# A new start order, some VectorE copies on ScalarE, earlier bank emptying, and second-layer weights stored already split

## The chip, the cores and the metric

The kernel runs on one core of one Trainium2 chip. The metric is device time in microseconds (us). Three runs of the kernel before took 1604.84 to 1608.25 us, with a median of 1606.85 us. Engines are named as in the profile: PE is TensorE, PEld its weight loads, DVE is VectorE, ACT is ScalarE, POOL is GpSimd, and SP is SyncE, which here only issues DMAs.

## What is computed

For each of 8 batches with 8 heads and 576 positions of 64 numbers, keys and values are first reduced to 32 memory slots, and the attention runs over those slots:

```
a   = softmax(phi over positions)             phi: 8 x 8 x 576 x 32
k_m = a^T k ;  v_m = a^T v                    32 x 64 per head
att = softmax(q k_m^T / 8) v_m                576 x 64 per head
x   = att, heads side by side                 4608 x 512
x   = relu(x w_in)^2 w_out                    first layer, 512 -> 2048 -> 512
h   = x w2_in ;  out = (h - tanh(h)) w2_out   second layer, same sizes
```

The inputs are 64-bit floats, handed over as pairs of 32-bit words.

## The kernel before, in words

**Numbers.** Every 64-bit weight tile of 128x512 is turned into 32-bit floats by `conv` (L131): one DMA of 512 KB into a `raw` (or `wo`) buffer, an ACT absolute value (L142), and four DVE operations (L144 to L148). A factor of a matmul is then split into a rounded high part and the low rest (`split`, L181: an ACT cast, then a subtraction on POOL or DVE), and each product is three matmuls: high by high, high by low, low by high.

**First layer.** Its work is a list of 256 steps (`seq`, L396). A step is one unit `u` of 288 tokens with one 128-row slice `f` of the 2048 hidden features. `step(s)` (L611) issues six matmuls of 128x288 for step s+3 (`l1_mm1`, L410), the relu, square and split for step s+2 (`l1_act`, L422 to L427), and twelve matmuls into four accumulator banks for step s (`l1_mm2`, L439 to L441). The attention is folded into the weights: `u_make` (L275) multiplies v_m into w_in, so that the first matmul takes the attention weights `aT` and the product `u`. At the last slice of a unit's part, `l1_out` (L447) copies the four accumulator banks out to `xs` tiles, two on ACT and two on DVE (L450), and stores or accumulates them to memory. Units 0 to 3 are done in parts of 4, 4 and 8 (or 8 and 8) slices, so that the first steps need few weights.

**What sets the order.** The work beside the steps is written as Python generators: `w..` converts a tile of w_in, `o..` a tile of w_out, `i..` is the memory-slot half of the attention (`att_a`, L198), `j..` the query half (`att_b`, L304), `u..` is `u_make`. Each advances one stage at a time, and each engine's queue is in the order in which the stages are issued. For the start, the order is the written list `ORDER` (L40), one word per stage; `S` in it is one step of the matmul pipeline. Up to about step 60 the list sets the order. After that `tick` (L371) advances every active generator once after each step, those that wait for nothing but emptying a PSUM bank (marked `"-"`) first. Two PSUM banks (`b`) serve all attention and `u_make` matmuls. Generators of batch b begin about 52 steps before its first unit.

**Second weights.** `w2_conv` (L461) converts the 32 tiles of the second layer's weights from step 40 on, one every 5.3 steps, and stores each as 128x512 floats (256 KB) in a memory scratch tensor. Near the end of the first layer `w2_load` (L473) loads each again into a scratch buffer and splits it (`split`, by DVE, for ten tiles by POOL). These loads, their scratch buffers and the loads of the first two token blocks (`x2_load`, L491) share the buffers `f2`, `f` and `raw`; SP issues the DMAs in order, and a DMA that waits for a buffer holds those behind it.

**Second layer.** 144 steps of 9 token blocks by 16 slices (L710): twelve matmuls of 128x512 (`l2_mm1`, L525) for step s+3, the function on ACT and DVE (L537 to L545), the split (L554 on ACT, L555 on POOL), and twelve matmuls for step s (`l2_mm2`, L569 to L571). After a block's last slice four banks are copied by ACT (L576) and stored by SP (L583) in pieces that follow the order of the output rows.

Of the kernel before, what the change touches and what calls it, by code (L numbers as in the profile page):

```python
# [37 lines left out]


ORDER = """  # L40
w22 o12 w02 o11 w10 i00 i01 j11 o2 o1 o3 i00 u01 o0 o6 w00 i01 o8 o0 w00 w02 w10 w02 i00 w00 w02 o0 i21 j00 i00 i00
w10 w01 w03 w13 w23 i00 w20 i00 w02 j01 o0 w03 w31 i00 i00 o9 i01 j01 w02 j01 o0 w01 o0 w01 i00 w00 i00 i00 o2 w03 i10
i01 w00 w10 w02 w12 i00 o4 w03 o0 w00 j01 o1 o12 i01 o0 i01 j01 i01 i20 w03 o1 j01 j01 i01 w01 o15 w13 o2 j00 o3 i01
i01 w01 o2 o2 w03 j00 u01 i01 w03 i01 i01 i01 o1 o4 w21 j01 w01 j01 j01 j01 o13 o12 j00 o1 w12 w00 w31 j01 j01 u00 u00
u00 i10 o7 o12 o2 w11 j20 o1 j00 o2 i10 w11 w30 o1 i11 j01 o4 j01 o3 j00 j01 w13 j00 j11 o1 o12 j01 j00 i11 i11 i10
i11 w31 i10 j00 i10 w11 j00 i10 o4 o12 o2 o12 o3 w10 w13 o4 i10 w03 j00 j00 w11 w12 o12 i10 o5 o5 j00 j00 o4 w01 o3 o4
i10 o4 j10 j00 w12 o14 j00 S j00 w13 i11 i10 i11 S i11 i11 o10 w12 o3 S o3 j11 i11 i10 i10 o5 w13 w00 j11 o3 S i11 o10
S i10 w10 i20 S o6 j11 w11 o4 o8 w32 i11 w11 w32 i11 i11 j11 w33 u10 S o5 o6 o7 j11 o7 j10 j11 j10 j11 o7 S w10 o5 o5
o6 j11 j11 o7 w12 u01 u01 u01 S w12 o5 o7 w20 o5 j11 o7 i20 o6 w02 u10 i20 j11 o8 j11 o10 j10 S u11 o6 u10 j21 j10 j11
w23 j10 o10 o10 w23 w23 o7 j10 o6 j11 j11 j10 S j10 j10 S o2 o8 j10 j10 w22 w22 o10 o8 j20 o6 w23 j10 w22 S w21 w23  # L50
w21 j10 w21 j10 o8 S S w20 w22 j20 j10 o11 w31 j10 S u11 w21 w31 S u11 w22 o8 j20 w21 S j20 S S o11 o9 j20 w20 S o11
w22 o10 o8 o9 o11 o11 o14 w20 o11 w20 o11 o14 w23 S j20 i20 w20 w21 j20 S u02 u02 o10 o9 o9 w23 w20 o13 S o13 u02 o9
u12 w11 o9 o12 w31 o14 j01 o14 u12 o14 S o13 o13 w10 u12 o9 i20 w13 w30 w32 w32 o10 S w32 w32 o13 w30 j20 o14 w22 w31
S w23 S w33 w30 w32 w22 w32 w21 S i21 w22 w23 w30 w33 w32 w30 S w30 w30 i21 i21 i20 i21 i20 S o13 o14 i20 w01 w33 S
w33 w31 i20 o15 i21 i21 w31 w33 S w20 w22 w30 w23 w32 w21 w20 w22 w32 w31 w20 w23 w30 w20 S i20 w32 i21 w33 i21 w20
w31 w31 o15 w21 i21 w30 w20 S i20 u03 w33 i20 u03 i21 S i20 w33 o13 j21 w22 u13 w23 w30 w31 w31 u03 w31 S w20 i21 i21
w22 i20 w31 w30 w30 w31 w31 S i21 w33 w20 w32 S w32 w21 w22 j20 w30 w33 i21 w20 w30 j20 w30 j21 w31 w10 w30 w33 S w23
w22 j21 w23 w20 S w32 w22 j20 i20 o15 w33 w31 w31 w32 i21 w20 w33 w21 o15 j21 w21 S w23 w32 j20 i20 i21 w22 w31 o15
w01 w30 w21 o15 w13 w23 i20 j21 w21 j20 j21 o15 j11 i20 i20 i20 j20 S i20 i21 i20 i20 u13 w21 i20 u13 S i21 i21 j21
j21 j20 i21 S j20 j21 j21 w32 w21 S j20 w33 S S S i20 j20 w21 S i20 w21 i20 i20 w23 w33 j20 i21 w33 j21 S i21 S S j20  # L60
j20 i21 i21 j20 i21 j20 j20 j20 j20 i00 j20 j20 S j21 j20 o6 j21 j20 w22 j21 S j21 w01 w33 j20 j21 w20 j21 j21 j20 i21
j20 j21 j21 j21 j21 j21 i21 j21 j20 j21 j21 j21 j21 j20 j20 S S i21 j01 S S S j21 S w32 S j20 j20 j21 j21 j20 j20 j21
j21 j21 S j21 j21 j21 j21 S j21 j21 S j20 j21 j21 j20 j20 S j20
"""


# [5 lines left out]
def moe_chain_kernel(ctx: ExitStack, tc: tile.TileContext, q, k, v, phi, w1i, w1o, w2i, w2o, out):  # L72
# [43 lines left out]
    def slot(p, shape, name, dt=F32):  # L116
        return p.tile(shape, dt, tag=p.name, name=name)
# [6 lines left out]
    def give(*rs):  # L124
        free.update(rs)
# [72 lines left out]
    def att_a(b, g, p_kv):  # L198
# [21 lines left out]
        yield "-"  # L220
        nc.vector.reduce_max(mx, t[:, :SP], axis=AX.X)
        dg = slot(p_f, [P, P], "dg")
        nc.vector.tensor_scalar(dg, ident, mx, None, op0=ALU.mult)
        give("b")
        yield "b"
        t = psum(ps_b, "mb")
# [36 lines left out]
            kt[b] = slot(a_kt, [P, H, M], f"kt{b}")  # L263
        yield "-"
        ts = t[:, :2 * P].rearrange("p (i h m) -> p i h m", i=2, h=4)
        nc.vector.tensor_copy(kt[b][:, heads], ts[:, 1])
        for o in range(2):
            nc.scalar.copy(vt[b][half(o), 2 * g:2 * g + 2], ts[half(o), 0, o::2])
        give("b")
# [34 lines left out]
    def att_b(b, o, p_q):  # L304
# [8 lines left out]
        for i in (0, 2):  # L313
            yield "b b"
            t = [psum(ps_b, f"qT{i}") for _ in range(2)]
            for n in range(2):
                for c in range(3):
                    nc.tensor.transpose(t[n][:, c * SP:(c + 1) * SP],  # L318
                                        qs[:, i + n, 2 * c:2 * c + 2, :].rearrange("p c d -> p (c d)"), ident[:SP, :SP])
            if i and p_q is a_q:  # L320
                give("q")
            yield "-"
            nc.scalar.copy(qt[:, i], t[0][:, :HT])
            nc.vector.tensor_copy(qt[:, i + 1], t[1][:, :HT])
# [45 lines left out]

    active, wants = [], {}  # L371

    def tick(new=()):
        active.extend(new)
        for gen in sorted(active, key=lambda gen: wants.get(gen, "") != "-"):
            need = collections.Counter(wants.get(gen, "").strip("-").split())
            if any(free[r] < n for r, n in need.items()):
                continue
            free.subtract(need)
            try:  # L380
                wants[gen] = next(gen) or ""
            except StopIteration:
                active.remove(gen)
# [87 lines left out]
    wi, ahead = {}, [3]

    def w2_load(m, f, p, p_x2f):  # L473
        of = "f2" if m == 0 else "f" if f < 8 else "raw"
        yield of
        x = slot(dict(f2=p_x2f, f=p_f, raw=p_raw)[of], [P, 512], "w2f")
        nc.sync.dma_start(x, w2_d[m, f])
        for _ in range(ahead[0]):
            yield
        if m:  # L480
            t = slot(p, [P, 2, 512], "wo", F32R)
            wo[2, f] = t[:, 0], t[:, 1]
        else:
            t = slot(p[f], [P, 2, 512], f"wi{f}", F32R)
            wi[f] = t.rearrange("p t (c n) -> p t c n", c=ET)
        yield from split(x, t[:, 0], t[:, 1], nc.gpsimd if m == 0 and f >= 6 else nc.vector)
        give(of)

    x2 = {}

    def x2_load(j, c, p_x2f):  # L491
        yield "f2 f2"
        ts = [slot(p_x2f, [P, 512], "x2f") for _ in range(2)]
        c0 = 512 * j
        while c0 < 512 * (j + 1):
            u, o = divmod(c0, HT)
# [61 lines left out]
    def l2_mm2(s):  # L558
# [7 lines left out]
        for i in range(4):  # L566
# [110 lines left out]
    for s in range(next_step[0], N1):  # L677
        if s == N1 - 22:
# [68 lines left out]
```

## Time and profile before

| what | value |
|---|---|
| median of 3 runs | 1606.85 us |
| the profiled execution's own time | 1608.32 us |
| its span, first to last instruction | 1606.2 us |
| mean granted TensorE clock | 0.995 |
| PE busy | 1535.8 us (96%) |
| PEld busy | 1334.0 us (83%) |
| DVE, ACT, POOL busy | 1071.6, 848.1, 620.6 us |

Busy time of an engine is the time in which at least one of its instructions is under way. A matmul's entry in the profile includes its way through the array, so successive ones overlap; the distance from one start to the next shows the rate. A wait names the engine, line and tile that waited, and what released it. In waits, the three numbers are the total in us, the count and the longest.

### The profile page before, as it was taken

Reading aid. Unit: us, or ns where it says so; the run is one execution under the profiler, and the core shown is the slowest. Engines: PE = TensorE matmul, PEld = TensorE weight load, DVE = VectorE, ACT = ScalarE, POOL = GpSimd, SP = SyncE. Lnnn points to the kernel's source line nnn. Section 1 sums busy time; section 2 is a strip of 40 time slices with the busy share of each in tenths; the row PEclk is TensorE's granted clock in tenths of the full one; section 3 lists DMA queues with packets and bytes.
Section 4 is the critical chain, followed back from the end, with each engine's and each line's share of the span. In section 5 each row is a group of like instructions: output and inputs, shape, how many; then the busy total and the mean of one; then the engine's idle time right before and its main releaser. Section 6 shows DMA issues by size and latency. Waiting matters only on the chain.

```text
span 1606.2 us, 26164 instructions
## 1 busy us (share of the span) xinstructions
PE 1535.8 (96%) x9904; PEld 1334.0 (83%) x9904; DVE 1071.6 (67%) x1508; ACT 848.1 (53%) x1765; POOL 620.6 (39%) x588
## 2 busy tenths in 40 slices
PE   4588999999999999999999999999999999999998
PEld 2477899998989899999978788888888888888887
DVE  6987445453535535430389788888979888888885
ACT  2466666666666665665755444445444444444443
POOL 2545465543534344443445333232424232333322
PEclk9999999999999999999999999999999999999999
DMA  9546655562644545321431100101010101010000
GB/s 304 161 130 157 212 134 158 152 197 79 208 141 151 174 156 171 109 108 35 122 106 46 42 12 20 34 1 43 11 40 14 41 12 42 11 43 11 19 9 27
DMA packets 89854, 146.28 MB, mean 91 GB/s; under 512 B 12416, under 2 KB 65664, under 8 KB 86656
## 3 DMA queue, kind: packets, MB, share of 16 engines
q1 hardware_dynamic: 86272, 141.07, 28.3%
q0 software_dynamic: 3456, 3.54, 1.7%
q8 instruction: 78, 1.28, 0.3%
q14 instruction: 48, 0.39, 0.1%
HBM read 109.58 MB, written 35.00 MB: 90 GB/s over the span
## 4 chain that ended last, share of the span: by engine, by line
PE 87%; DVE 4%; DMA 4%; ACT 2%; issue 1%; SPq 0%; POOL 0%; ACTq 0%; DVEq 0%; POOLq 0%
PE h L525 23%; PE h L410 12%; PE o L569 8%; PE o L571 8%; PE o L570 8%; PE acc L441 8%; PE acc L439 8%; PE acc L440 8%; PE u L283 2%; PE vkm L244 1%; DMA kv<-in_v 1%; DMA kv<-in_k 1%; PE qT L318 1%; DMA raw<-in_moe_w_out 1%; DMA raw<-in_moe_w_in 1%
## 5 line engine op out<-in xcount | busy, mean ns | idle before, releaser
L525 PE MATMUL h<-x,wi 128*128 128x512 f32 x1728 | 415.4, 390 | 2.1 <-POOL x L508 2.1
L555 POOL TENSOR_TENSOR gl<-pl,gh 128x512 fp32r<-128x512 f32 x144 | 190.3, 1321 | 528.7 <-PE o L570 482.8
L525 PEld LDWEIGHTS h<-x,wi 128*128 128x128 f32 x1728 | 324.1, 188 | 70.2 <-POOL x L508 3.1
L427 POOL TENSOR_TENSOR g<-gg,g 128x288 fp32r<-128x288 f32 x256 | 223.1, 886 | 365.0 <-ACT g L426 277.2
L439 PE MATMUL acc<-g,wo 128*128 128x288 f32 x1024 | 302.1, 295 | 3.4 <-DVE xs L450 3.2
L441 PE MATMUL acc<-g,wo 128*128 128x288 f32 x1024 | 302.7, 296 | 0.0
L440 PE MATMUL acc<-g,wo 128*128 128x288 f32 x1024 | 302.3, 295 | 0.0
L537 ACT ACTIVATE u<-h 128x512 f32<-128x512 f32 x144 | 86.1, 598 | 392.0 <-PE h L525 391.9
L410 PE MATMUL h<-aT,u 128*128 128x288 f32 x1536 | 261.2, 306 | 8.2 <-ACT aT L362 3.5
L410 PEld LDWEIGHTS h<-aT,u 128*128 128x128 f32 x1536 | 218.9, 191 | 41.9 <-issue 21.3
L571 PE MATMUL o<-wo,gl 128*128 128x512 f32 x576 | 225.8, 392 | 2.4 <-POOL gl L555 2.4
L569 PE MATMUL o<-wo,gh 128*128 128x512 f32 x576 | 226.0, 392 | 1.1 <-ACT gh L554 1.1
L570 PE MATMUL o<-wo,gh 128*128 128x512 f32 x576 | 225.6, 392 | 0.0
L439 PEld LDWEIGHTS acc<-g,wo 128*128 128x128 f32 x1024 | 193.2, 189 | 4.1 <-DVE xs L450 3.7
L441 PEld LDWEIGHTS acc<-g,wo 128*128 128x128 f32 x1024 | 193.3, 189 | 0.0
L440 PEld LDWEIGHTS acc<-g,wo 128*128 128x128 f32 x1024 | 193.1, 189 | 0.0
L540 DVE SCALAR_TENSOR_TENSOR pl<-u 128x512 f32<-128x512 f32 x144 | 100.1, 695 | 95.4 <-ACT u L537 95.4
L422 ACT ACTIVATE gg<-h 128x288 f32<-128x288 f32 x256 | 104.9, 410 | 103.7 <-PE h L410 98.3
L544 DVE SCALAR_TENSOR_TENSOR pl<-pl,u 128x512 f32<-128x512 f32 x144 | 148.5, 1031 | 0.0
L545 DVE COPY_PREDICATED pl<-m,th 128x512 f32<-128x512 int32 x144 | 139.0, 965 | 4.9
L571 PEld LDWEIGHTS o<-wo,gl 128*128 128x128 f32 x576 | 108.9, 189 | 26.8 <-POOL gl L555 4.1
L569 PEld LDWEIGHTS o<-wo,gh 128*128 128x128 f32 x576 | 108.7, 189 | 24.5 <-ACT gh L554 1.9
(85 smaller groups left out, 1993.0 us busy)
## 6 DMA issues: line engine op xcount, KB each, us to landing
w<-w_d SPq DMA_DIRECT2D x24, 1024.0 KB, 5.7
raw<-in_moe_w_out SPq DMA_DIRECT2D x32, 512.0 KB, 5.6
raw<-in_moe_w_in SPq DMA_DIRECT2D x32, 512.0 KB, 5.4
kv<-in_v SPq DMA_DIRECT2D x64, 144.0 KB, 4.6
kv<-in_k SPq DMA_DIRECT2D x64, 144.0 KB, 4.3
q<-in_q SPq DMA_DIRECT2D x16, 576.0 KB, 5.6
x_d<-xs SPq DMA_DIRECT2D x64, 144.0 KB, 3.4
w_d<-wf SPq DMA_DIRECT2D x32, 256.0 KB, 2.2
```

What stands on the lines that cost most here:

```text
L410: nc.tensor.matmul(t[:, :HT], uu[:, w, o, c], at[u // 2][:, x, o, u % 2 * HT:u % 2 * HT + HT], start=(n == 0), stop=(n == 5))
L427: nc.gpsimd.tensor_tensor(gl, gg, gh.bitcast(F32), op=ALU.subtract)
L439: nc.tensor.matmul(o, wh[:, c], gh, start=(f == a), stop=False)
L440: nc.tensor.matmul(o, wh[:, c], gl, start=False, stop=False)
L441: nc.tensor.matmul(o, wl[:, c], gh, start=False, stop=(f == z - 1))
L525: nc.tensor.matmul(t, wi[f][:, w, c, :], x, start=(n == 0), stop=(n == 11))
L544: stt(pl, pl, A0, u, op0=ALU.add, op1=ALU.mult)
L545: nc.vector.copy_predicated(pl, m.bitcast(I32), th)
L555: nc.gpsimd.tensor_tensor(lo, pl, hi.bitcast(F32), op=ALU.subtract)
L569: nc.tensor.matmul(o, gh[:, c], wh, start=(f == 0), stop=False)
L570: nc.tensor.matmul(o, gh[:, c], wl, start=False, stop=False)
L571: nc.tensor.matmul(o, gl[:, c], wh, start=False, stop=(f == FT - 1))
```

## The change

Five things change. (1) `ORDER` is a new list: 779 words in place of 716, with the same pieces and 66 `S` in both. (2) Copies move from DVE to ACT: the diagonal `dg` in `att_a` (L223), the `kt` copy (L266), the second `qt` copy (L324), and, for units 0 to 3, the two of four `xs` copies (L450) that DVE had. (3) `empty()` runs between `l1_act` and `l1_mm2` of a step: generators whose next stage empties a PSUM bank are advanced there, ahead of the `xs` copies of a unit's end, and not a second time in the same step's `tick`. (4) `w2_conv` splits the tile where it is converted (ACT cast, DVE subtraction) and stores both parts (512 KB); `w2_load` is one DMA into the final buffer, with no scratch buffer and no split, and ten tiles of each matrix are loaded later; the second token block's `x2_load` takes `raw` buffers in place of `f2`. (5) For the last two output banks, the copy is halved between ACT and DVE, and the second DMA of each bank is issued from ACT.

```diff
--- before.py
+++ after.py
@@ -38,29 +38,31 @@
 
 
 ORDER = """
-w22 o12 w02 o11 w10 i00 i01 j11 o2 o1 o3 i00 u01 o0 o6 w00 i01 o8 o0 w00 w02 w10 w02 i00 w00 w02 o0 i21 j00 i00 i00
...
+w00 w00 o11 w02 i01 o0 w11 i00 u01 o2 w10 o8 w22 o12 j00 i00 i01 w02 w01 w02 i00 o0 i21 i00 i00 o3 j11 o0 w00 i00 w03
...
 """
 
 
@@ -220,7 +222,7 @@
         yield "-"
         nc.vector.reduce_max(mx, t[:, :SP], axis=AX.X)
         dg = slot(p_f, [P, P], "dg")
-        nc.vector.tensor_scalar(dg, ident, mx, None, op0=ALU.mult)
+        nc.scalar.activation(dg, ident, AF.Copy, scale=mx)
         give("b")
         yield "b"
         t = psum(ps_b, "mb")
@@ -263,7 +265,7 @@
             kt[b] = slot(a_kt, [P, H, M], f"kt{b}")
         yield "-"
         ts = t[:, :2 * P].rearrange("p (i h m) -> p i h m", i=2, h=4)
-        nc.vector.tensor_copy(kt[b][:, heads], ts[:, 1])
+        nc.scalar.copy(kt[b][:, heads], ts[:, 1])
         for o in range(2):
             nc.scalar.copy(vt[b][half(o), 2 * g:2 * g + 2], ts[half(o), 0, o::2])
         give("b")
@@ -321,7 +323,7 @@
                 give("q")
             yield "-"
             nc.scalar.copy(qt[:, i], t[0][:, :HT])
-            nc.vector.tensor_copy(qt[:, i + 1], t[1][:, :HT])
+            nc.scalar.copy(qt[:, i + 1], t[1][:, :HT])
             give("b", "b")
         while not {("a", b, g) for g in range(2)} <= done:
             yield
@@ -370,9 +372,22 @@
 
     active, wants = [], {}
 
+    emptied = []
+
+    def empty():
+
+        for gen in [gen for gen in active if wants.get(gen, "") == "-"]:
+            advance(gen)
+            emptied.append(gen)
+            if wants[gen] == "end":
+                active.remove(gen)
+
     def tick(new=()):
         active.extend(new)
+        done_now, emptied[:] = list(emptied), []
         for gen in sorted(active, key=lambda gen: wants.get(gen, "") != "-"):
+            if gen in done_now:
+                continue
             need = collections.Counter(wants.get(gen, "").strip("-").split())
             if any(free[r] < n for r, n in need.items()):
                 continue
@@ -447,7 +462,7 @@
     def l1_out(u, a):
         outs = [slot(p_t, [P, HT], "xs") for _ in range(ET)]
         for e in range(ET):
-            (nc.vector.tensor_copy if e % 2 else nc.scalar.copy)(outs[e], acc[u][e][:, :HT])
+            (nc.vector.tensor_copy if e % 2 and u > 3 else nc.scalar.copy)(outs[e], acc[u][e][:, :HT])
         yield
         for e in range(ET):
             if a:
@@ -456,7 +471,7 @@
                 nc.sync.dma_start(x2_d[u][e], outs[e])
 
 
-    w2_d = {(m, f): p_d.tile([P, 512], F32, name=f"w2_d{m}_{f}") for m in range(2) for f in range(FT)}
+    w2_d = {(m, f): p_d.tile([P, 2, 512], F32, name=f"w2_d{m}_{f}") for m in range(2) for f in range(FT)}
 
     def w2_conv(m, f):
         if m:
@@ -464,33 +479,35 @@
         else:
             src = w2i.rearrange("(c p) f -> p c f", p=P)[:, :, f * 2 * P:(f + 1) * 2 * P]
         x = yield from conv(src, None, None, 3)
-        yield
-        nc.sync.dma_start(w2_d[m, f], x)
+        yield "raw"
+        t = slot(p_raw, [P, 2, 512], "w2s", F32R)
+        yield from split(x, t[:, 0], t[:, 1], nc.vector)
         give("f")
-
-    wi, ahead = {}, [3]
-
-    def w2_load(m, f, p, p_x2f):
-        of = "f2" if m == 0 else "f" if f < 8 else "raw"
-        yield of
-        x = slot(dict(f2=p_x2f, f=p_f, raw=p_raw)[of], [P, 512], "w2f")
-        nc.sync.dma_start(x, w2_d[m, f])
-        for _ in range(ahead[0]):
-            yield
+        yield
+        nc.sync.dma_start(w2_d[m, f], t.bitcast(F32))
+        give("raw")
+
+    wi = {}
+
+    def w2_load(m, f, p):
+        t = slot(p if m else p[f], [P, 2, 512], "wo" if m else f"wi{f}", F32R)
+        nc.sync.dma_start(t.bitcast(F32), w2_d[m, f])
         if m:
-            t = slot(p, [P, 2, 512], "wo", F32R)
             wo[2, f] = t[:, 0], t[:, 1]
         else:
-            t = slot(p[f], [P, 2, 512], f"wi{f}", F32R)
             wi[f] = t.rearrange("p t (c n) -> p t c n", c=ET)
-        yield from split(x, t[:, 0], t[:, 1], nc.gpsimd if m == 0 and f >= 6 else nc.vector)
-        give(of)
+        yield
 
     x2 = {}
 
     def x2_load(j, c, p_x2f):
-        yield "f2 f2"
-        ts = [slot(p_x2f, [P, 512], "x2f") for _ in range(2)]
+        of = "raw" if j == 1 else "f2 f2"
+        yield of
+        if j == 1:
+            t = slot(p_raw, [P, 2, 512], "x2r")
+            ts = [t[:, i] for i in range(2)]
+        else:
+            ts = [slot(p_x2f, [P, 512], "x2f") for _ in range(2)]
         c0 = 512 * j
         while c0 < 512 * (j + 1):
             u, o = divmod(c0, HT)
@@ -507,7 +524,10 @@
         for i in range(2):
             nc.gpsimd.tensor_tensor(lo[:, i], ts[i], hi[:, i].bitcast(F32), op=ALU.subtract)
             x2[j, c + i] = hi[:, i], lo[:, i]
-            give("f2")
+            if j != 1:
+                give("f2")
+            elif i:
+                give("raw")
             yield
 
     N2 = NB * FT
@@ -573,14 +593,20 @@
                 if i % 2 == 0:
                     acc["t"] = slot(p_raw, [P, 2, 512], "osb")
                 t = acc["t"][:, i % 2]
-                nc.scalar.copy(t, o)
+                last = j == NB - 1 and i > 1
+                if last:
+                    nc.scalar.copy(t[:, :256], o[:, :256])
+                    nc.vector.tensor_copy(t[:, 256:], o[:, 256:])
+                else:
+                    nc.scalar.copy(t, o)
                 c0 = 512 * j + P * i
                 a = c0
                 while a < c0 + P:
                     u, r = divmod(a, HT)
                     cc, p0 = divmod(r, SP)
                     n = min(SP - p0, c0 + P - a)
-                    nc.sync.dma_start(out_v[u // 2, 2 * cc + u % 2, p0:p0 + n, :], t[a - c0:a - c0 + n, :])
+                    q_out = nc.scalar if last and a > c0 else nc.sync
+                    q_out.dma_start(out_v[u // 2, 2 * cc + u % 2, p0:p0 + n, :], t[a - c0:a - c0 + n, :])
                     a += n
 
 
@@ -611,6 +637,7 @@
     def step(s):
         l1_mm1(s + 3)
         l1_act(s + 2)
+        empty()
         if s >= 0:
             l1_mm2(s)
 
@@ -683,11 +710,8 @@
             p_x2.append(pool("x2_0", 4, **tile_wise))
             p_wi += [pool(f"wi{f}", 1, **tile_wise) for f in range(6)]
             for f in range(FT):
-                if f < 6:
-                    at_step(s + 2 * f, w2_load(0, f, p_wi, p_x2f))
-                else:
-                    at_step(N1 - 8 + f, w2_load(0, f, p_wi, p_x2f))
-                at_step(N1 - 16 + f, w2_load(1, f, p_wo, p_x2f))
+                at_step(s + 2 * f if f < 6 else N1 - 4 + f, w2_load(0, f, p_wi))
+                at_step((N1 - 15 if f < 6 else N1 - 3) + f, w2_load(1, f, p_wo))
             for c in (0, 2):
                 at_step(N1 - 9 + c, x2_load(0, c, p_x2f))
                 at_step(N1 + 4 + c, x2_load(1, c, p_x2f))
@@ -700,7 +724,6 @@
             p_wi += [pool(f"wi{f}", 1, side="right", **tile_wise) for f in range(FT - 1, 5, -1)][::-1]
         new, plan[s] = plan.get(s, ()), ()
         tick(new)
-    ahead[0] = 1
     tick(plan.pop(N1, ()))
     plan = {k - N1 - 3: g for k, g in plan.items() if k >= N1}
     def l2_ready(s):
```

## Rows read from the trace of the kernel before

**Rows 1.** The page: span, and busy time by engine over the whole span.

```profile
span 1606.2 us, 26164 instructions
...
PE 1535.8 (96%) x9904; PEld 1334.0 (83%) x9904; DVE 1071.6 (67%) x1508; ACT 848.1 (53%) x1765; POOL 620.6 (39%) x588
```

**Rows 2.** Stretches: length, busy us of PE, PEld, DVE, ACT, POOL, granted clock, DMA, GB/s.

```profile
0.00:50.00 50.00, 23.28 (x182) 12.98 (x182) 36.82 (x62) 15.10 (x28) 14.00 (x18) 1.00 0.93 283
50.00:100.00 50.00, 33.21 (x299) 27.79 (x300) 45.61 (x67) 26.66 (x59) 22.18 (x22) 1.00 0.47 151
100.00:150.00 50.00, 43.95 (x333) 38.88 (x332) 39.81 (x58) 31.96 (x73) 34.05 (x33) 0.97 0.54 126
150.00:200.00 50.00, 48.17 (x438) 43.17 (x437) 26.44 (x48) 31.31 (x73) 22.15 (x25) 0.97 0.69 214
250.00:650.00 400.00, 392.28 (x3516) 365.54 (x3515) 186.70 (x298) 248.74 (x571) 173.63 (x198) 1.00 0.50 155
```

**Rows 3.** Waits of PE from 75 to 200 us, first and last of eleven.

```profile
PE acc L439 <- DVE xs L450: 3.2, 2, 2.0
...
PE acc L439 <- ACT xs L450: 0.2, 1, 0.2
```

**Rows 4.** The same view of stretches, two short ones of the start.

```profile
135.00:140.00 5.00, 5.00 (x27) 5.00 (x28) 1.09 (x3) 1.27 (x3) 4.71 (x5) 0.66 1.07 208
160.00:165.00 5.00, 3.53 (x18) 3.07 (x18) 2.74 (x6) 4.71 (x12) 1.61 (x2) 0.81 0.77 233
```

**Rows 5.** Instruction groups by line: count, busy us, mean ns, idle time before; DVE copies.

```profile
L450 DVE COPY xs<-acc 128x288 f32<-128x288 f32 x44 | 19.6, 454 | 78.6 <-PE acc L441 39.0 <-POOL g L427 33.0 <-issue 6.6
...
L324 DVE COPY qt<-qT 128x288 f32<-128x288 f32 x32 | 14.4, 451 | 43.4 <-PE qT L318 43.4
...
L223 DVE TENSOR_SCALAR dg<-ident,mx 128x128 f32<-128x128 f32 x16 | 6.0, 375 | 0.8
L266 DVE COPY kt<-vkmT 128x128 f32<-128x128 f32 x16 | 4.6, 290 | 36.9 <-PE vkmT L259 36.9
```

**Rows 6.** The same view: the other two of the four copies, on ACT.

```profile
L450 ACT COPY xs<-acc 128x288 f32<-128x288 f32 x44 | 17.1, 398 | 33.5 <-PE acc L441 33.5
```

**Rows 7.** One wait of PE over the whole span.

```profile
PE m1T L219 <- DVE u L288: 7.3, 5, 1.5
```

**Rows 8.** Order of time, 365 to 371 us: start, length, instruction, idle time before it.

```profile
365.36 1.09 PE L283 MATMUL u<-w,vt 64*32 64x512 f32 x16
...
368.31 0.46 DVE L450 COPY xs<-acc 128x288 f32<-128x288 f32 x1 [3.31 <-issue]
...
369.00 1.08 ACT L287 CAST u<-u 128x512 fp32r<-128x512 f32 x2
...
370.46 0.28 PE L219 MATMUL m1T<-ident,m 96*128 96x96 f32 x1 [1.46 <-DVE u L288]
```

**Rows 9.** Order of time, PE, where the second layer begins.

```profile
805.90 11.12 PE L525 MATMUL h<-x,wi 128*128 128x512 f32 x48
```

**Rows 10.** The chain that ended last: start, length, what.

```profile
893.03 3.42 POOL x L508 x2
901.57 2.74 PE h L525 x12
...
1587.03 2.72 PE h L525 x12
```

**Rows 11.** Groups by line, DVE: the second weights' subtraction before the second layer.

```profile
L184 DVE TENSOR_TENSOR wo<-w2f,wo 128x512 fp32r<-128x512 f32 x16 | 15.6, 990 | 16.3 <-ACT wo L182 16.3
```

**Rows 12.** DMA issues: KB each, median us to landing.

```profile
w<-w_d SPq DMA_DIRECT2D x24, 1024.0 KB, 5.7
raw<-in_moe_w_out SPq DMA_DIRECT2D x32, 512.0 KB, 5.6
```

**Rows 13.** Order of time, the end of the span: ACT's last copies, SP's last issues.

```profile
1598.63 2.62 ACT L576 COPY osb<-o 128x512 f32<-128x512 f32 x4 [2.85 <-PE o L571]
...
1599.24 4.06 SPq L583 DMA_DIRECT2D out<-osb  x8
```

More of the change, by code (lines that the diff above doesn't have):

```diff
@@ L40 @@
 ORDER = """
-w22 o12 w02 o11 w10 i00 i01 j11 o2 o1 o3 i00 u01 o0 o6 w00 i01 o8 o0 w00 w02 w10 w02 i00 w00 w02 o0 i21 j00 i00 i00
[L42 to L60, printed above, removed]
@@ L61 @@
-j20 i21 i21 j20 i21 j20 j20 j20 j20 i00 j20 j20 S j21 j20 o6 j21 j20 w22 j21 S j21 w01 w33 j20 j21 w20 j21 j21 j20 i21
-j20 j21 j21 j21 j21 j21 i21 j21 j20 j21 j21 j21 j21 j20 j20 S S i21 j01 S S S j21 S w32 S j20 j20 j21 j21 j20 j20 j21
-j21 j21 S j21 j21 j21 j21 S j21 j21 S j20 j21 j21 j20 j20 S j20
+w00 w00 o11 w02 i01 o0 w11 i00 u01 o2 w10 o8 w22 o12 j00 i00 i01 w02 w01 w02 i00 o0 i21 i00 i00 o3 j11 o0 w00 i00 w03
+w20 w02 i00 w02 w00 o3 w10 i00 w01 w01 o0 w03 w03 w12 w10 i00 i01 j01 w02 j00 o1 o2 i00 o0 j00 i01 w00 w02 j01 j01 i20
@@ new lines @@
+w00 w13 i00 i00 i00 o12 w00 w03 o0 o4 w31 o1 i01 i10 i01 o4 w23 o0 j00 o9 j01 i01 w03 o1 j01 i01 j01 w01 w10 j01 o2
+i01 w01 u00 o4 o15 i01 o2 i01 u01 o12 o2 i01 w03 w21 i01 i01 w03 o1 w01 j01 j01 o4 w13 o13 o0 j01 o4 o1 j20 w11 w00
+u00 u00 j01 j01 w11 j01 o2 o4 w21 i00 o6 u00 o2 o12 w11 w21 o1 o3 w12 o4 o1 o4 j01 j00 j00 j01 o1 j00 w30 j00 w31 j00
+w21 o12 o7 j01 i10 j01 i10 i10 o2 i10 w11 j00 i10 i11 o12 j01 o3 o2 j00 i10 o12 i10 w10 j11 w31 w31 i11 o0 w02 j00 o12
+w12 i10 w03 i11 j00 j00 o5 o4 o5 o3 w13 o3 i10 j00 j00 o14 S i10 o10 i11 w12 i11 w13 o5 i10 j00 j11 S i11 w00 w12 i11
@@ new lines @@
+w01 S S o3 i11 w20 w11 o3 i11 i10 o5 i01 i20 j11 o10 o3 S i11 S j11 w13 w10 w11 o7 i10 o7 w13 o7 w32 w00 w32 o6 j11
+w33 o8 i11 i11 o7 i11 u10 S u12 j11 j11 j11 o6 j10 S o7 o5 o7 o5 w10 j11 j11 o6 j10 w12 S u01 o5 j10 u01 o5 j11 w12
+u10 i20 o7 u01 o10 o6 j10 o6 j10 o8 j11 S u11 o7 o6 u10 o10 j11 w23 j01 j11 w21 j21 o6 w23 o10 j10 o1 j10 u12 j11 j11
+j10 S j10 j20 o2 w23 S o8 j10 o10 w23 o8 o12 j10 w21 j10 w01 j10 S o8 w22 j10 j10 w22 S S o11 w20 w22 w21 w23 j10 j10
+S w21 j20 u11 S i20 w21 u11 o8 w22 w02 o11 S j20 S w20 S j20 w31 o11 o10 o1 o10 w22 w22 j20 o9 o14 o11 w11 S o11 w31
@@ new lines @@
+w31 w20 o11 w20 w23 o8 w21 o14 S w20 o9 S u02 j20 i20 u02 w23 w32 o9 o9 j20 w20 o13 S w33 o10 u02 o13 o9 o14 o11 u12
+o9 j01 o14 o12 w23 u12 S j11 o13 o13 u12 w23 o9 i20 w13 w10 w23 w30 w32 w32 o14 w32 S w21 w31 w33 w23 w32 o14 w21 w22
+o13 j20 w30 w30 w23 S i21 w32 S w32 w30 S w33 j01 S i21 i21 i20 w33 w23 w30 i21 w33 w30 w31 w30 w20 i20 S o14 i20 w01
+j20 o13 S w00 w33 w20 w23 i21 w31 i20 w21 w31 w31 w31 o15 w33 w31 S w31 j10 j20 w02 w31 S w22 w30 w30 i20 w22 i21 i21
+w23 w23 j20 o15 S i21 i21 i20 u03 w33 w30 i20 u03 i21 j10 w21 o12 w03 S i20 S w20 i21 i21 i20 u13 w23 w23 o13 j21 u03
@@ new lines @@
+w33 i21 w31 w31 j01 w33 w20 w22 w30 w20 w22 w31 i20 S w20 w32 w32 j20 w20 i21 S w20 j21 j20 w10 j20 w20 j21 w30 w31
+w33 o15 w32 w22 i20 S o14 o2 i21 S w21 i21 w30 w22 w20 w30 w33 w01 o12 w32 w31 w22 w21 j21 o15 w13 S w31 w01 i21 w32
+j20 o15 w21 w20 o15 w32 j10 o15 w30 w30 w21 j21 j20 w22 j21 w33 i10 j11 S w21 w22 w20 j20 w10 u13 w32 w32 u13 w21 w20
+S j20 w31 w32 w22 S w31 w21 w21 j20 S j21 o6 j11 w30 j20 w22 w21 j21 j21 S w31 S S w33 w30 j20 j21 j20 S o15 j20 j01
+j20 j20 j20 i00 j20 w33 S j20 S S w23 j20 o3 j21 j21 i20 j20 j00 j20 j21 S j20 w03 j20 j20 w01 j01 j21 j20 S j20 j21 S
@@ L64 @@
+i20 w32 o0 j20 w20 j00 j20 j20 S w33 S j21 i21 j21 j21 S i21 j21 j21 i21 j20 j21 w22 S j20 S o7 j21 i20 i21 j21 i20
+j20 j20 i20 i21 S i21 i20 i21 j21 j21 j21 j20 j20 i20 j21 i21 j21 j21 i20 j21 i21 i21 j21 i21 i21 S j21 i20 j21 j21
+i20 w32 j21 j21 S j21 j20 w21 w33 S j21 S i20 j20 w11 i20 j21 j21 j21 j21
 """
@@ L466, in w2_conv @@
         x = yield from conv(src, None, None, 3)
+        yield "raw"
+        t = slot(p_raw, [P, 2, 512], "w2s", F32R)
+        yield from split(x, t[:, 0], t[:, 1], nc.vector)
+        give("f")
         yield
-        nc.sync.dma_start(w2_d[m, f], x)
-        give("f")
-    wi, ahead = {}, [3]
-    def w2_load(m, f, p, p_x2f):
-        of = "f2" if m == 0 else "f" if f < 8 else "raw"
-        yield of
-        x = slot(dict(f2=p_x2f, f=p_f, raw=p_raw)[of], [P, 512], "w2f")
-        nc.sync.dma_start(x, w2_d[m, f])
-        for _ in range(ahead[0]):
-            yield
+        nc.sync.dma_start(w2_d[m, f], t.bitcast(F32))
[4 more added lines that the diff above has]
+        nc.sync.dma_start(t.bitcast(F32), w2_d[m, f])
         if m:
-            t = slot(p, [P, 2, 512], "wo", F32R)
             wo[2, f] = t[:, 0], t[:, 1]
         else:
-            t = slot(p[f], [P, 2, 512], f"wi{f}", F32R)
             wi[f] = t.rearrange("p t (c n) -> p t c n", c=ET)
-        yield from split(x, t[:, 0], t[:, 1], nc.gpsimd if m == 0 and f >= 6 else nc.vector)
-        give(of)
+        yield
     x2 = {}
     def x2_load(j, c, p_x2f):
-        yield "f2 f2"
-        ts = [slot(p_x2f, [P, 512], "x2f") for _ in range(2)]
+        of = "raw" if j == 1 else "f2 f2"
[5 more added lines that the diff above has]
+            ts = [slot(p_x2f, [P, 512], "x2f") for _ in range(2)]
         c0 = 512 * j
```

## The prediction

> **What bounds the kernel now.** I read the page first: PE is busy 96% of 1606.2 us, its weight loads 83%, DVE 67%, ACT 53% [rows 1]. So PE bounds the kernel on average, and a gain has to come from the places where PE stands still or has not started. The view of stretches shows where those are. In the first 50 us PE is busy 23 us, in the next 50 us 33, then 44 and 48; from 250 to 650 us it is busy 392 of 400 [rows 2]. While PE is short of work, DVE is the engine that is full: 37, 46 and 40 of 50 us in the first three stretches, against 15, 27 and 32 for ACT [rows 2]. The list of PE's waits from 75 to 200 us says the same in detail: eleven kinds, 3.2 us for the first and 0.2 for the last, 11.7 us together, and most name a DVE copy [rows 3]. Two short dips of the granted clock come on top: the clock reads 0.66 and 0.81 over 5 us [rows 4], its lower level of 1.2 GHz for a part of each stretch and 2.4 GHz in the rest. The missing shares, 0.34 and 0.19 of 5 us, are 2.6 us of PE time.
>
> The steady first layer has one wait that repeats: the transpose `m1T` waits for the `u` subtraction, five times, 7.3 us [rows 7]. In order of time it is plain why [rows 8]: at a unit's end the `xs` copies stand on ACT and DVE ahead of the `u` cast and subtraction, which empty the two `b` banks. The `u` matmuls end at 366.45, a copy of `xs` starts at 368.31, the casts start only at 369.00, and PE stands still for 1.46 us before `m1T`.
>
> Then the change of layers. PE's first second-layer matmul starts at 805.90 [rows 9]. The steady rate comes from the chain: from 901.57 to 1587.03 lie 126 steps [rows 10], 5.440 us each, so a group of twelve matmuls is 2.72. The group at 901.57 is the eighteenth of L525, with 17 such groups and 14 of the output product ahead of it: 31 x 2.72 = 84.3 us, where 95.7 went by. The change of layers loses 11.3 us, in two places: the first steps, where the splits of the second weights stand between the steps' own DVE work (0.99 us each for a `wo` tile [rows 11]), and a later place where POOL splits the second token block too late, at 893.03 [rows 10].
>
> **The change, part by part.**
>
> *Copies off DVE, and the new list.* Up to about step 31, within the first 200 us, the change takes from DVE: 8 `qt` copies at 0.451, 4 `kt` at 0.290, 4 `dg` at 0.375 and, at six part ends of units 0 to 3, 12 `xs` at 0.454 [rows 5]: 3.6 + 1.2 + 1.5 + 5.4 = 11.7 us. I counted the pieces of both lists: the conversions ahead of each step are nearly the same, so the new list mainly fits the lighter DVE. Where DVE is full, its queue's work is the time: I take 11.7 us, which is also what PE waits after 75 us [rows 3]. Bounds: a loss of 5 us, if the new list orders worse and half of what ACT takes over shows; and a gain of 17.4 us, if all 11.7 us of waits go, the 2.6 us of clock with them, and the four attention halves ahead of the first step start it 3.1 us earlier (4 x 0.451, 2 x 0.290, 2 x 0.375 [rows 5]). On ACT the same copies cost about 28 x 0.4 = 11 us by its own `xs` copy, 0.398 [rows 6]; ACT has 95 us free of the first 200 [rows 2], so this is covered. Without that cover they would sit in front of the relu of the next step, 0.4 us a copy.
>
> Here a rule speaks against the move. The trace has both engines doing the same copy out of a bank: 0.454 us on DVE, 0.398 on ACT [rows 5, 6]. The Trainium skill, "ScalarE: Activation LUTs", Rules for kernel authors, says to use VectorE and not ScalarE for simple element work, DVE being up to about three times faster in bf16 for single-source operations. By that rule the first term would be gone; for this 32-bit copy out of a bank the rows do not agree.
>
> *Banks emptied first.* `empty()` puts the casts and subtractions of [rows 8] ahead of the `xs` copies. The `u` matmuls are done 2.5 us before the casts begin now, so the casts can run ahead of the `xs` copies. Gain 7.3 us [rows 7]; bounds 0 and 7.3. What is late next are the `xs` copies; the next unit's first accumulation needs the first bank only after six more matmuls and `m1T`, about 1 us of cover.
>
> *Second weights split where converted.* Removed at the change of layers: 32 ACT casts, 22 DVE and 10 POOL subtractions, and the sharing of `f2` and `raw`. I expect all 11.3 us back. Bounds: 11.3 and 4, the second being the case that the token block stays late. Added: 32 casts and 32 DVE subtractions, at most 0.99 us each [rows 11], between steps 40 and 214. DVE is idle for 213 and ACT for 151 of the 400 us in the middle [rows 2], so I cost them at nothing; as the pattern (5.3 steps) nearly repeats every 32 steps, a collision with an emptying would repeat in five batches, so the bound is 5 x 0.99 = 5 us. A second `raw` buffer per conversion lengthens its stay; the batches begin 52 steps ahead, which covers it. On SP, stores of 512 KB follow the subtraction by a step and wait for little; the loads of the late tiles stand one of each matrix per second-layer step, issued three steps or more ahead of use. The load of 1024 KB takes 5.7 us [rows 12], so 512 KB is well inside 16 us.
>
> *The end.* ACT's four copies end at 1601.25; SP issues eight stores one after another from 1599.24 for 4.06 us [rows 13]. Two of the eight go to ACT's queue, so SP ends about 2 x 0.5 us earlier, and the half copies save about 0.2; ACT's last half copy stands behind one issue, which takes 0.1 back. I take 1.1 us, bounds 0.4 and 1.7.
>
> **Sum.** 11.7 + 7.3 + 11.3 + 1.1 = 31.4 us. The profiled execution took 1608.3 us itself, 2.1 more than its span, and 1.5 us over the median 1606.85; less 31.4 it is 1576.9, or 1575.4 from the median. I say 1576.
>
> **The rivals.**
> - *The start gives nothing.* If ACT, DMA or the latency from stage to stage sets the start, the first term is 0: 1588 us. For it: DMA is 0.93 busy in the first 50 us [rows 2], and PE waits there for chains across engines. Against it: DVE is 91% busy from 50 to 100 us [rows 2]. By the rule of the Trainium skill above the time would be this one too.
> - *The layers' change stays late.* If the second block's split or the loads still come late, 7 to 11 us stay: about 1585.
> - *The wait moves.* `xs` copies behind the casts hold the next unit's accumulation for as long as `m1T` waited: 7.3 us less, 1583.
> - *Slower: the doubled loads starve the second layer.* Twenty loads of 512 KB, two per step, are due in its first ten late steps. A 512 KB load took 5.6 us in the crowded start [rows 12]. If they land one after another at that price, two cost 11.2 us against a step of 5.44: 5.8 late per step, 58 in ten steps, less three steps of lead, 16: 42 us late, 1618 us. It decides from 2.72 us per load upwards. Against it: the median of 1024 KB is 5.7 us [rows 12], and DMA moved 283 GB/s in the first 50 us [rows 2], which is 1.9 us for 512 KB.
> - *The parts do nothing.* If DVE's relief is taken up by added splits in the middle (5 us), `m1T` stays and the layers' change gains only 4: about 1607, no change.
>
> **How the numbers follow.** Forecast 0.62, a start without gain 0.18, a late change of layers 0.07, a moved wait 0.06, slower 0.04, nothing 0.03. At the one end, 17.4 + 7.3 + 11.3 + 1.7 = 37.7, which is 1569 from the median; 1566 leaves room for an earlier first step than I can price. At the other end, no gain at the start and every other part at its lower half, 7.3 - 5 + 7 + 0.4 = 9.7, is 1597; what is worse is left out with the slower case and the last one. A measurement of this kernel can tell about 0.2% (3.2 us) from no change. Faster by more than that: 0.93; within it: 0.03; slower: 0.04.
>
> **What would show it.** Right: the waits of `acc` for `xs` and of `m1T` for `u` are gone; the first steps of the second layer are 5.44 us apart at once, and POOL ends no wait there; DVE is busy some 12 us less in the first 200 us, and the first-layer steps stand 10 us or more earlier by 280 us. Wrong: a new wait of PE for ACT's copies (`qt`, `xs`, `dg`) in the first 200 us, second-layer matmuls that wait for a DMA, or a first step no earlier than before.

## The result and the profile after

The changed kernel takes 1582.11 us (median of 4 runs, 1580.14 to 1583.17), the kernel before 1607.55 beside it. The ratio is 0.9841 with a 95% interval of 0.9823 to 0.9860: 25.4 us, or 1.6%, faster. Beside other kernels it was measured once more at 1581.0 us, with a ratio of 0.9834 (0.9818 to 0.9849).

The page of the kernel after, span and busy time, as in [rows 1]:

```profile
span 1578.4 us, 26135 instructions
...
PE 1523.9 (97%) x9904; PEld 1329.9 (84%) x9904; DVE 1043.0 (66%) x1436; ACT 868.1 (55%) x1849; POOL 605.2 (38%) x578
```

Its stretches, with the columns of [rows 2]:

```profile
0.00:50.00 50.00, 21.49 (x182) 12.89 (x182) 33.61 (x57) 19.02 (x39) 12.51 (x18) 1.00 0.84 276
50.00:100.00 50.00, 38.10 (x346) 31.95 (x340) 42.12 (x64) 32.27 (x76) 29.33 (x28) 1.00 0.51 158
100.00:150.00 50.00, 42.95 (x338) 38.11 (x338) 39.69 (x48) 33.85 (x79) 31.15 (x31) 0.97 0.65 158
150.00:200.00 50.00, 48.50 (x453) 45.50 (x453) 24.96 (x40) 35.23 (x86) 24.48 (x28) 1.00 0.59 182
250.00:650.00 400.00, 400.00 (x3602) 373.13 (x3593) 196.12 (x292) 275.85 (x649) 178.54 (x204) 1.00 0.56 176
```

Where the time came from is read from the first second-product matmul of chosen steps in the two profiled executions. Their spans are 27.8 us apart, 2.4 us more than the medians, because the execution after is the shortest of its four and the one before is longer than the median:

| place | before, us | after, us | gained so far |
|---|---|---|---|
| first layer, step 0 | 74.7 | 69.0 | 5.7 |
| step 31 | 183.5 | 176.4 | 7.1 |
| step 63 | 275.8 | 267.6 | 8.2 |
| step 240 | 771.0 | 754.6 | 16.5 |
| second layer, step 0 | 816.9 | 800.4 | 16.5 |
| its step 15 | 909.6 | 882.0 | 27.6 |
| its last step | 1597.8 | 1570.2 | 27.6 |
| end | 1606.2 | 1578.4 | 27.8 |

So the start gave 8.2 us, the middle 8.2, the change of layers 11.1 and the end 0.3. The 8.2 of the start and the 0.3 of the end are single readings; both vary from execution to execution, as the runs below show.

**Middle.** A unit's end in the kernel after, in order of time, answers to [rows 8]:

```profile
355.50 1.09 PE L285 MATMUL u<-w,vt 64*32 64x512 f32 x16
...
356.68 1.07 ACT L289 CAST u<-u 128x512 fp32r<-128x512 f32 x2 [1.25 <-PE u L285]
357.30 1.29 DVE L290 TENSOR_TENSOR u<-u,u 128x512 fp32r<-128x512 f32 x2 [4.93 <-ACT u L289]
...
358.50 0.45 DVE L465 COPY xs<-acc 128x288 f32<-128x288 f32 x1
...
358.99 0.25 PE L221 MATMUL m1T<-ident,m 96*128 96x96 f32 x1
```

The casts begin 0.1 us after the `u` matmuls instead of 2.5, the `xs` copies come behind them, and `m1T` has no idle time before it.

**Change of layers.** The chain of the kernel after answers to [rows 9, 10]:

```profile
789.60 10.99 PE h L545 x48
803.30 2.72 PE h L545 x12
...
1559.46 2.72 PE h L545 x12
```

Four groups and one output product from 789.60 would end at 803.2; the next group starts at 803.30, and the 139 steps to 1559.46 take 5.440 us each. PE has no wait at all from 780 us on.

**Waits of PE** from 75 to 200 us, the first two and the last of ten, against [rows 3]:

```profile
PE h L425 <- ACT gg L437: 3.7, 3, 2.0
PE u L285 <- ACT qt L325: 2.4, 1, 2.4
...
PE acc L454 <- ACT xs L465: 0.2, 1, 0.2
```

They are 12.4 us together, hardly other than the 11.7 before. The waits for DVE's copies are gone, and waits for ACT's have come.

### The profile page after: what moved, and what is told of

Read it like the earlier page. It is cut to its first block, busy times and chain, and to the rows that moved or that the text cites. A ratio compares the mean times of both kernels' runs of the same rounds, so it can differ in the third digit from the quotient of the medians.

```text
span 1578.4 us, 26135 instructions
## 1 busy us (share of the span) xinstructions
PE 1523.9 (97%) x9904; PEld 1329.9 (84%) x9904; DVE 1043.0 (66%) x1436; ACT 868.1 (55%) x1849; POOL 605.2 (38%) x578
## 4 chain that ended last, share of the span: by engine, by line
PE 91%; DVE 3%; DMA 3%; ACT 2%; issue 1%; POOL 1%; SPq 0%; ACTq 0%; POOLq 0%
PE h L545 25%; PE h L425 13%; PE o L591 8%; PE o L590 8%; PE o L589 8%; PE acc L456 8%; PE acc L455 8%; PE acc L454 8%; PE u L285 2%; PE vkm L246 1%; PE qT L320 1%; DMA w_d<-w 1%; PE sc L334 1%; DVE wf L150 1%; DMA raw<-in_moe_w_in 1%
```

## The experiments

Each kernel ran beside the kernel before, and kernels are compared by their ratios to it. The changed kernel's is 0.9834 to 0.9841, and 0.001 is 1.6 us. Step 39 is read for the start, as it is the last one before the conversions of the second weights begin.

**The old list, all else as changed.**

```diff
-w00 w00 o11 w02 i01 o0 w11 i00 u01 o2 w10 o8 w22 o12 ...
+w22 o12 w02 o11 w10 i00 i01 j11 o2 o1 o3 i00 u01 o0 ...
```

> The changed kernel with the old written order for the start, all else as changed. The changed kernel has its step 39 at 201.3 us, the kernel before at 209.3, and 1582.1 us in all. Theory A (the relief of DVE by the moved copies makes the gain of the start, the new list hardly any): step 39 within 2 us of 201.3, and 1582 to 1584 us in all. Theory B (the list makes it): step 39 near 209, and about 1590 us.

Measured: 1589.2 us, ratio 0.9890 (0.9875 to 0.9906), step 39 at 211.0 us. By its numbers it is theory B: with the old list, relieving DVE gives nothing at the start. The stretches of this kernel show DVE lighter than before, 40.6 and 34.8 us against 45.6 and 39.8 in [rows 2], and PE no busier:

```profile
50.00:100.00 50.00, 33.89 (x280) 29.04 (x280) 40.60 (x56) 28.50 (x66) 22.56 (x22) 0.97 0.47 147
100.00:150.00 50.00, 43.26 (x349) 38.94 (x349) 34.77 (x47) 35.10 (x83) 34.22 (x33) 0.97 0.52 120
```

The waits of DVE in its first 200 us, one row of this kernel and then the same row of the kernel before, say where the time went: DVE waits for the absolute values that ACT issues ahead of a conversion.

```profile
DVE wf L144 <- ACT wf L142: 16.8, 6, 6.8
```

```profile
DVE wf L144 <- ACT wf L142: 4.7, 2, 3.9
```

**The new list with the copies on DVE.**

```diff
-nc.scalar.activation(dg, ident, AF.Copy, scale=mx)
+nc.vector.tensor_scalar(dg, ident, mx, None, op0=ALU.mult)
-nc.scalar.copy(kt[b][:, heads], ts[:, 1])
+nc.vector.tensor_copy(kt[b][:, heads], ts[:, 1])
-nc.scalar.copy(qt[:, i + 1], t[1][:, :HT])
+nc.vector.tensor_copy(qt[:, i + 1], t[1][:, :HT])
-(nc.vector.tensor_copy if e % 2 and u > 3 else nc.scalar.copy)(outs[e], ...)
+(nc.vector.tensor_copy if e % 2 else nc.scalar.copy)(outs[e], ...)
```

> The changed kernel with the four moved copies (dg, kt, second qt, xs of units 0 to 3) back on DVE, new list kept. Theory A (DVE's load sets the start): step 39 some 6 to 9 us later than 201.3, about 1589 to 1591 us in all. Theory B (the list makes the gain): step 39 within 2 us of 201.3, 1582 to 1584 us.

Measured: 1598.2 us, ratio 0.9946 (0.9933 to 0.9958), step 39 at 218.1 us. That is beyond both theories: the new list with the old copies is 9 us worse at step 39 than the kernel before. Neither list nor copies make the gain alone.

**Without the early emptying.**

```diff
     def step(s):
         l1_mm1(s + 3)
         l1_act(s + 2)
-        empty()
```

> The changed kernel without the emptying of banks between the activation and the second matmuls of a step. Theory A (the five stalls of m1T at unit ends came from the xs copies standing ahead): the wait of m1T for the u subtraction is back with five times 1.5 us, 1.65 us per place in the step distances, 8 us in all, 1590 us. Rival (the moved copies on ACT removed the stall, not the order): no such wait, 1582 us.

Measured: 1589.3 us, ratio 0.9891 (0.9877 to 0.9904). The row of [rows 7] is back, on the new lines:

```profile
PE m1T L221 <- DVE u L290: 7.6, 5, 1.8
```

Theory A holds: 8 to 9 us by the ratios. From step 63 to 240 this kernel takes 497.1 us, the changed one 487.0. Of these 10.1 us, 8.5 lie in the five places; 1.6 lie behind the first of them, where the granted clock read 0.66 from 270 to 275 us, part of that at its lower level of 1.2 GHz.

**Second weights stored unsplit, split late.**

```diff
...
-        yield "raw"
-        t = slot(p_raw, [P, 2, 512], "w2s", F32R)
-        yield from split(x, t[:, 0], t[:, 1], nc.vector)
+        yield
+        nc.sync.dma_start(w2_d[m, f], x)
...
-        nc.sync.dma_start(t.bitcast(F32), w2_d[m, f])
...
+        yield from split(x, t[:, 0], t[:, 1], nc.gpsimd if m == 0 and f >= 6 else nc.vector)
...
```

> The changed kernel with the second weights stored unsplit, and loaded and split late, as before (scratch buffers and old due steps too). Theory A (the splits on DVE and POOL and the shared buffers cost the change of layers 11 us, and the added splits in the middle cost nothing): 11 us more, 1593 us, and steps 64 to 240 at the same distance as in the changed kernel. Rival (the splits in the middle cost up to 5 us there): the middle gets up to 5 us shorter, and only 6 us are lost in all, 1588 us.

Measured: 1589.6 us, ratio 0.9891 (0.9877 to 0.9904). From step 255 of the first layer to step 15 of the second it takes 102.5 us, 8.3 more than the changed kernel; the kernel before took 105.3. Its waits of PE there:

```profile
PE h L540 <- POOL x L523: 3.1, 2, 2.4
PE o L586 <- POOL gl L570: 1.7, 2, 0.9
```

From step 63 to 240 it takes 487.0 us, as the changed kernel: the 32 added splits in the middle cost nothing. Theory A holds in its places; of the 11 us, 8.3 are shown by removal. The kernel before had two stretches behind its stalls that were in part at 1.2 GHz (granted clock 0.90 and 0.76 from 835 to 845 us, 0.70 and 0.96 from 895 to 905), this one had one (0.88 and 0.78 from 875 to 885). By the shares missing from each 5 us, such a stretch costs about 1.7 us. The edit puts back the late splits, the scratch buffers and the due steps together, so it does not say which of them costs how much.

**The changed kernel again.** No edit.

> The changed kernel itself, once more, beside the others of this call. Its step 39 has been at 201.3 us, and in two other kernels with the same order up to step 40 at 199.5 and 203.7. All theories: about 1582 us, step 39 between 199 and 204. A step 39 outside of that would mean that the start varies more from run to run than the parts of it that are to be told apart.

Measured: 1581.0 us, step 39 at 204.1. Four more kernels have the same order of work on every engine up to step 39 (without the early emptying, with the late splits, and the last two below), and in these six executions step 39 lies at 199.5 to 204.1 us: the start varies by 4.5 us between executions. Differences at step 39 under that are not read below. It also follows that neither the emptying nor the second weights touch the start; its gain belongs to the list and the copies.

**The old list with the copies on DVE.** The edits of the first two together.

> The changed kernel with the old list and the four copies back on DVE. Old list with moved copies gave 211 us at step 39, new list with DVE copies 218. Theory A (list and copies fit each other: each list loses with the other's copies): step 39 near 209, as in the kernel before, 1590 us in all. Theory B (the old list is worse by itself, and the copies on ACT helped it): step 39 at 214 or later, 1594 us or more.

Measured: 1589.7 us, ratio 0.9888 (0.9872 to 0.9904), step 39 at 208.3. Theory A. With this the square is full:

| | copies on DVE | copies on ACT |
|---|---|---|
| old list | 0.9888 | 0.9890 |
| new list | 0.9946 | 0.9834 |

**Only dg back on DVE**, the first of the four edits above.

> The changed kernel with only dg back on DVE. Theory A (dg on ACT makes ACT wait for DVE's maximum and costs; with the new list it is laid around): within 2 us of the changed kernel, up to 2 us better, 1580 to 1583 us. Theory B (the new list needs DVE relieved of each of the four): step 39 some 2 to 4 us later, 1584 to 1586 us.

Measured: 1580.4 us, ratio 0.9837 (0.9821 to 0.9854). Theory A: `dg` on either engine is the same.

**The old list, with dg alone on DVE.**

> The old list, with qt, kt and xs on ACT and only dg on DVE, all else as changed. With dg on ACT too the old list had step 39 at 211.0, ACT waited 12.7 us for DVE's maximum ahead of dg, and DVE waited 18.1 us for the absolute value of a conversion behind it. Theory A (dg on ACT, in an order that was laid out for dg on DVE, makes the two wait for each other in turn and eats the relief): that wait of ACT is gone, step 39 at 203 to 206, 1583 to 1585 us. Theory B (the old list does not use the relief of DVE whatever dg does): step 39 at 209 to 212, 1588 to 1590 us.

Measured: 1590.3 us, ratio 0.9894 (0.9879 to 0.9909), step 39 at 213.5. Theory B: `dg` was not what ate the relief. The row above (DVE waiting for the absolute values) still reads 12.6 us in this kernel.

**Only xs back on DVE**, the last of the four edits, and **only qt and kt**, the two in the middle.

> The changed kernel with only the xs copies of units 0 to 3 back to two on ACT and two on DVE. With all four copies on DVE the new list cost 16 us. Theory A (a copy that the new list has on ACT stands on DVE behind long conversions, and the accumulators it must empty hold up the next unit; so xs is the one that counts): 8 us or more later, 1589 to 1596 us, and PE waits for xs or DVE waits for the accumulators. Theory B (what counts is the sum of DVE's work, shared out by time): xs is half of the moved time, so about half of the 16 us, 1587 to 1590, and the attention's copies the other half.

> The changed kernel with only qt and kt back on DVE. Theory A (xs is the copy that counts): within 3 us of the changed kernel, 1581 to 1584 us. Theory B (DVE's summed work counts): 5 to 8 us later, 1586 to 1589 us.

Measured: `xs` 1586.1 us, ratio 0.9862 (0.9845 to 0.9878), 4.5 us more than the changed kernel; `qt` and `kt` 1592.8 us, ratio 0.9906 (0.9890 to 0.9922), 11.6 us more. Both theories missed the split. By DVE time up to step 31, `xs` are 5.4 us and `qt` with `kt` 4.8, so each microsecond of the attention's copies counts more than twice. Order of time in the kernel with `qt` and `kt` on DVE, and then the same places in the changed kernel:

```profile
35.78 0.69 PE L261 MATMUL vkmT<-ident,vn 128*128 128x128 f32 x2 [1.74 <-ACT vn L255]
...
37.30 0.28 DVE L268 COPY kt<-vkmT 128x128 f32<-128x128 f32 x1
37.62 0.42 ACT L270 COPY vt<-vkmT 64x64 f32<-64x64 f32 x2 [1.89 <-DVE kt L268]
...
49.06 2.63 PE L320 MATMUL qT<-ident,q 96*128 96x96 f32 x12 [6.83 <-DVE u L290]
```

```profile
33.70 0.69 PE L261 MATMUL vkmT<-ident,vn 128*128 128x128 f32 x2 [1.04 <-ACT vn L255]
...
34.43 0.27 ACT L268 COPY kt<-vkmT 128x128 f32<-128x128 f32 x1 [0.78 <-PE vkmT L261]
...
46.04 2.56 PE L320 MATMUL qT<-ident,q 96*128 96x96 f32 x12 [6.83 <-DVE u L290]
```

By 49 us the attention's chain is 3 us late. Of these, 2.1 us are lost ahead of `vkmT`: `q` lands 0.8 us later, and `qt` copies stand between DVE's conversions. The `kt` copy, which stands behind a conversion in DVE's queue and for which ACT waits, adds 0.8 us. Step 0 begins at 75.4 us instead of 69.0; how the rest of that is lost was not followed, and `qt` and `kt` were not tried apart.

**The end with whole copies.**

```diff
-                last = j == NB - 1 and i > 1
-                if last:
-                    nc.scalar.copy(t[:, :256], o[:, :256])
-                    nc.vector.tensor_copy(t[:, 256:], o[:, 256:])
+                last = j == NB - 1 and i > 2
+                if j == NB - 1 and i == 2:
+                    nc.vector.tensor_copy(t, o)
```

> The changed kernel with whole copies at the end in place of halves: bank 2 by DVE, bank 3 by ACT, and only the last bank's second store issued from ACT. In the changed kernel DVE's halves wait for ACT's halves of the same bank, and ACT's last half waits behind a store whose data DVE had yet to copy; the end after the last matmul's start is 5.7 us. Theory A (these two waits eat the gain of the halves): the two halves' serial run is gone, the last store is issued 0.6 to 0.9 us earlier, the end is 5.0 us after the last matmul's start. Rival (landing and closing work set the end whatever the copies do): unchanged within 0.2 us. In all 1581 us either way.

The end of the changed kernel, in order of time:

```profile
1571.67 3.38 SPq L609 DMA_DIRECT2D out<-osb  x6
1572.42 0.37 ACT L598 COPY osb<-o 128x256 f32<-128x256 f32 x1
1572.82 0.42 DVE L599 COPY osb<-o 128x256 f32<-128x256 f32 x1 [5.36 <-ACT osb L598]
1573.28 0.56 ACTq L609 DMA_DIRECT2D out<-osb  x1
1573.88 0.37 ACT L598 COPY osb<-o 128x256 f32<-128x256 f32 x1 [1.09 <-DVE osb L599]
1574.28 0.42 DVE L599 COPY osb<-o 128x256 f32<-128x256 f32 x1 [1.03 <-ACT osb L598]
1574.74 0.38 ACTq L609 DMA_DIRECT2D out<-osb  x1
```

And with whole copies:

```profile
1571.92 3.60 SPq L608 DMA_DIRECT2D out<-osb  x7
1572.67 0.69 DVE L598 COPY osb<-o 128x512 f32<-128x512 f32 x1 [4.94 <-PE o L591]
...
1573.97 0.38 ACTq L608 DMA_DIRECT2D out<-osb  x1
```

Measured: 1580.7 us, ratio 0.9829 (0.9813 to 0.9844), not told apart from the changed kernel. ACT's last store is issued 1.0 us sooner after the last matmul's start, but SP now has seven stores in a row, and its last is issued as late as ACT's was before; the end is 5.6 us after that start, against 5.6 and 5.7 in the two profiled executions of the changed kernel. The two waits are gone and nothing is gained: the rival in its outcome. That SP's issuing now sets the end fits this, but no run took a store off SP to test it.

**The second block through f2.**

```diff
-        of = "raw" if j == 1 else "f2 f2"
+        of = "f2 f2"
...
```

> The changed kernel with the second token block loaded through the f2 buffers again, in place of raw. Theory A (the block came late because the weight loads shared f2 and because of their splits, both of which are gone): no change, second-layer steps 5.44 us apart throughout, 1581 to 1582 us. Rival (f2 alone, with three buffers for two pairs, makes it late): a stall of up to 4 us at steps 13 and 14.

Measured: 1579.0 us, ratio 0.9823 (0.9804 to 0.9842), the second layer's first 15 steps in 81.6 us, as in the changed kernel. Theory A: the move to `raw` does nothing once the weights no longer use `f2`.

## Why the prediction was right, and where not

It said 1576 us within 1566 to 1597, faster; 1582.1 lies inside. Two of the four terms, the banks and the second weights, had the right mechanism. The largest term, the start, had the right sign with a wrong reason, so that the time fell inside the range is in part luck. In ratios, taking out the list and the copies costs 0.0054, the emptying and the second weights 0.0050 to 0.0057 each, 0.0154 to 0.0168 together; the whole change is 0.0159 to 0.0166, so no large part is left unexplained.

*The start* was the step that failed in its reason. It said "Where DVE is full, its queue's work is the time: I take 11.7 us", and that "the new list mainly fits the lighter DVE". The start gave 8.2 us in one profiled execution, 6.1 in the other, and 8.7 by the ratios (0.9888 less 0.9834). But 0.9888 and 0.9890 show that taking the same copies off DVE in the old order gives nothing. In that kernel DVE was busy 135.4 us of the first 200 against 148.7 before, and the freed time became waits, most of them for ACT's part of the conversions. A DVE that is 91% busy was not a DVE whose length sets the end. Nor did the waits go away that the term was set equal to: PE's waits from 75 to 200 us were 11.7 us and are 12.4. Of the 8.2 us, 5.7 are there at step 0, ahead of those waits, where the prediction had 3.1 us at most and only in its upper bound. It also misread the waits when it said that most name a DVE copy: beside the first line of [rows 3] only these two of the eleven do, 5.4 us of the 11.7 together.

```profile
PE sc L332 <- DVE qt L324: 1.5, 1, 1.5
PE u L283 <- DVE qt L324: 0.7, 1, 0.7
```

Its own signs came out mixed: the new wait of `u` for ACT's `qt` copy is one of those that it named for being wrong, step 63 stands 8.2 us earlier and not 10, and DVE is busy 8.3 us less in the first 200, not 12. What the runs show in place of the step is that list and copies work only together: the new list with the copies on DVE is 9 us slower than the old one. That the start is set by where pieces stand in queues that run in a written order, and not by DVE's sum, is the reading that fits this; that the attention's copies count more than twice their time fits it too and is shown by removal. Which pieces of the new list make the rest of its gain was not tried.

*The rule of the Trainium skill* ("ScalarE: Activation LUTs", Rules for kernel authors), by which the first term would have been gone, names relu, max, min, add and mul and gives its factor for bf16. Taken over to these 32-bit copies out of a bank it did not hold: with the new list the copies on ACT are worth 18 us by the ratios (0.9946 less 0.9834), with the old list nothing.

*Banks emptied first*: 7.3 us forecast, 8.2 in the profile, 8.5 in the five places by removal; the stall costs about 1.65 us a place, not the 1.46 of its wait alone.

*Second weights*: 11.3 forecast, 11.1 in the profile, 8.3 by removal with the rest of the change in place. The cover named for the added splits was there: the middle did not change. The fear of the doubled loads had its place but not its price. In two stretches after the change of layers the DMA engines are full, and PE does not wait:

```profile
795.00:800.00 5.00, 5.00 (x24) 4.14 (x23) 4.84 (x9) 3.91 (x7) 1.67 (x1) 1.00 1.00 389
800.00:805.00 5.00, 5.00 (x24) 4.14 (x23) 4.79 (x9) 2.22 (x4) 1.66 (x1) 1.00 0.99 340
```

SP issued the twenty loads between 791 and 814 us, within five steps and not ten, so the lead of the later ones was longer than the three steps that the prediction counted.

*The end*: 1.1 us forecast, 0.3 in the profile, and no gain is shown: in the twelve profiled executions with half copies the end comes 5.6 to 6.3 us after the last matmul's start, in the one of the kernel before 6.0. SP's last issue ends 0.7 us sooner after that start, not 1.0. The step that failed besides is "the half copies save about 0.2; ACT's last half copy stands behind one issue, which takes 0.1 back". The halves of a bank ran one after the other, and ACT's last half waited 1.09 us, as its queue held a store whose data DVE had yet to copy. About 0.8 of that is the store's: with whole copies ACT's last copy starts 0.4 us after the last matmul's start, here 1.2. The Trainium skill, "PSUM — Partial Sum Buffer", PSUM bank collisions raise a hardware error, says that two engines must be kept from the same bank and the same 32 partitions at the same time, also when both only read and when they read different columns. The trace agrees, in that each DVE half waits for the ACT half of its bank (1572.82 after 1572.42 and 0.37).

No version tried is shown to beat the changed kernel: 0.9823 and 0.9829 lie within its interval.

## What to carry to other kernels

An engine that is busy nine tenths of a stretch need not be the bound: its waits can grow when its work shrinks. With queues in a written order, test the order and the sharing of work together, since each may lose alone what both gain. A copy that a chain of other engines waits for can cost more than its length, by where it stands in the queue (11.6 us for 4.8 here). At a unit's end, empty first what the next piece of work needs soonest.

## What the runs showed of the hardware that was not expected

Six executions with the same order of work up to step 39 reached it at 199.5 to 204.1 us, a spread of 4.5 us with no change in the program there; its cause is open. From 795 to 820 us the DMA engines moved 340 to 415 GB/s, mostly for loads of 512 KB in rows of 4 KB, above the 283 GB/s of the first 50 us before [rows 2].
